# First MLP of a fused attention and two-MLP kernel: the integer addition of the weight conversion from GpSimd to VectorE, r*r on ScalarE in all blocks, and conversion steps left out at three f-steps of a block

## The chip, the cores and the metric

One core of a Trainium2 chip. The metric is the device time of one execution in microseconds, the median of repeated runs. The kernel before takes 1394.09 us (three runs, 1392.44 to 1394.47).

## The reference, cut to what matters

Inputs are float32; the weights arrive as float64 and are taken apart on the chip.

```python
scores = scale * x @ state.T          # per batch and head; S = 512, Ns = 32, D = 64
xread  = softmax(scores)  @ state
sread  = softmax(scores.T) @ x
x = concat([xread, sread])            # 4608 tokens of 512
h = x @ w_in                          # first MLP, 512 -> 2048
r = maximum(h, 0.0)
g = r * r
x = g @ w_out                         # 2048 -> 512
...                                   # second MLP: elu between two products
```

## The kernel before, in words

The program has two stages. The first holds the attention and the first MLP, the second (from about 725 us) the second MLP in a form with seven products. The change touches the first stage alone.

The first stage runs over nine blocks `b`: eight of 512 token columns (kind "X", one batch each) and one of 256 state columns (kind "S"). A block runs over 16 f-steps `i` of 128 hidden units. In an f-step TensorE multiplies for `h` (`s1_x`: six matmuls, each factor split into a high and a low fp32r part, so three matmuls per product), then `relu2` makes the square, and two f-steps later (`LAG = 2`) twelve matmuls add the square times the weights `v1` into four accumulators `acc`. At the end of a block `L400` on ScalarE and `L398` on VectorE copy the four `acc` tiles into `o` (two buffers), in turn ScalarE, VectorE, ScalarE, VectorE, and SyncE stores each.

`relu2` (L355 to L365) is: `r = relu(h)` on ScalarE (L357); `g = r*r` in fp32, on ScalarE in block 0 (L360) and on VectorE in all other blocks (L362); `gs[HI] = r*r` rounded to fp32r on ScalarE (L364); `gs[LO] = g - gs[HI]` on VectorE (L365). `r` and `g` have one buffer each, `gs` has three.

The weights are converted from float64 to float32 by integer work on their two 32-bit words (`convert`, L126 to L144): ScalarE scales the high word (L136) and the low word (L137), VectorE clamps and shifts (L139, L140), GpSimd adds the low word as a 32-bit integer (L142), and VectorE puts the sign in (L144). Each piece is 128x512; there are 64: 16 of `w1`, 16 of `v1`, 16 each of `w2` and `v2`. `w1` and `v1` are used in the first MLP and are converted before and during block 0. `w2` and `v2` go in pairs through `conv_pair`, which also forms sums of quarters (L177 to L181), splits them (L188 on ScalarE, L189 on VectorE) and stores them to HBM for the second stage.

`raw` has four buffers (`RAW = 4`): a piece is loaded by SyncE (L122) when an earlier piece has been given up by L144. `convert` and its callers are generators; each call of `next_conv` takes every conversion in progress one `yield` further. Calls stand in the f-steps: two per f-step in block 0, one in each of the f-steps 2 to 17 of the blocks 1 to 7, until nothing is left to convert. Beside them stand the steps of the attention for the next block (`at_scores`, `at_soft1`, ... , `emit_m`).

The order of instructions on each engine is not that of the code: a scheduler sets it when the program is built. Each engine then works through its own queue in order, and SyncE's queue of DMA issues too.

Of the kernel before, what the change touches and what calls it, by code (L numbers as in the profile page):

```python
# [13 lines left out]
AF = mybir.ActivationFunctionType  # L14
ALU = mybir.AluOpType
# [23 lines left out]
def attn_mlp_kernel(ctx: ExitStack, tc: tile.TileContext, xt, xn, st, w1, v1, w2, v2, outx, outs):  # L39
# [13 lines left out]
    nc = tc.nc  # L53
# [44 lines left out]
    if True:  # L98
# [28 lines left out]
        def convert(name, i, out):  # L127

            t = raw.pop((name, i))
            low, high = t[:, :, 0], t[:, :, 1]
            bits = out.bitcast(I32)
            with tc.issue_after(pace[0].ins) if name in ("w2", "v2") else nullcontext():
                nc.scalar.activation(out=out, in_=high.bitcast(F32), func=AF.Copy, scale=2.0 ** -112)  # L136
            nc.scalar.activation(out=low, in_=low.bitcast(U32), func=AF.Copy, scale=2.0 ** -29)  # L137
            yield
            nc.vector.tensor_scalar(out=out, in0=out, scalar1=CLAMP, scalar2=-CLAMP, op0=ALU.min, op1=ALU.max)  # L139
            nc.vector.tensor_single_scalar(out=bits, in_=bits, scalar=3, op=ALU.logical_shift_left)  # L140
            yield
            nc.gpsimd.tensor_tensor(out=bits, in0=bits, in1=low, op=ALU.add)  # L142
            yield
            nc.vector.scalar_tensor_tensor(out=bits, in0=high, scalar=SIGN, in1=bits, op0=ALU.bitwise_and, op1=ALU.bitwise_or)  # L144

# [206 lines left out]
            for k in range(KC):  # L352
                mm3(ps, (w[:, HI, k], w[:, LO, k]), (op[:, HI, k], op[:, LO, k]), k == 0, k == KC - 1)

        def relu2(ps, n, act):  # L355
            r = g_p.tile([P, n], F32, name="r", tag="r")
            pace[:] = [nc.scalar.activation(out=r, in_=ps, func=AF.Relu)]  # L357
            g = g_p.tile([P, n], F32, name="g", tag="g")
            if act:
                nc.scalar.activation(out=g, in_=r, func=AF.Square)  # L360
            else:
                nc.vector.tensor_tensor(out=g, in0=r, in1=r, op=ALU.mult)  # L362
            gs = gs_p.tile([P, 2, n], F32R, name="gs", tag="gs")
            nc.scalar.activation(out=gs[:, HI], in_=r, func=AF.Square)  # L364
            nc.vector.tensor_tensor(out=gs[:, LO], in0=g, in1=gs[:, HI].bitcast(F32), op=ALU.subtract)  # L365
            return gs

        def block(kind, b, op, bg, nxt):


            n = S if b < B else NST
            gs, acc = {}, []
            for i in range(FC + LAG):
                if i < FC:
                    ps = ps_s1.tile([P, n], F32, name="h", tag="s1")
                    if kind == "X":
                        s1_x(b, op, i, ps)
                    else:
                        s1_s(op, i, ps)
                    gs[i] = relu2(ps, n, kind == "X" and b == 0)  # L380
                for todo in bg.get(i, ()):
                    todo()
                if i == FC - 1:
                    following = nxt()
                f = i - LAG
                if f < 0:
                    continue
                if f == 0:
                    acc = [ps_acc.tile([P, n], F32, name="acc", tag="acc") for _ in range(KC)]
                g = gs.pop(f)  # L390
                w = wo_t["v1", f]
                for k in range(KC):
                    sl = slice(k * P, (k + 1) * P)
                    mm3(acc[k], (w[:, HI, sl], w[:, LO, sl]), (g[:, HI], g[:, LO]), f == 0, f == FC - 1)
            for k in range(KC):
                o = o_p.tile([P, n], F32, name="o", tag="o")
                if k % 2:
                    nc.vector.tensor_copy(out=o, in_=acc[k])  # L398
                else:
                    nc.scalar.activation(out=o, in_=acc[k], func=AF.Copy)  # L400
                nc.sync.dma_start(out=x2d[b][:, k], in_=o)
            return following
# [20 lines left out]
        op = operand_x(0)  # L423

        for b in range(B + 1):
            bg = {i: [] for i in range(FC + LAG)}

            def at(i, fn, *a):
                bg[i].append(lambda: fn(*a))

            nb = b + 1
            if b == 0:
                for i in range(FC - 1):
                    at(i, next_conv)
                    at(i, next_conv)
                at(3, emit_m, 0, 1)
                at(7, emit_m, 0, 2)
                at(11, emit_m, 0, 3)
                at(1, at_sread, 0)
                at(2, at_srt, 0)  # L440
                at(0, load_x, 1)
                at(3, load_xn, 1)
            elif b < B:
                at(1, emit_m, b, 1)
                at(5, emit_m, b, 2)
                at(9, emit_m, b, 3)
                for i in range(2, 18):
                    at(i, next_conv)
            if nb < B:
                at(1 if b else 6, at_scores, nb)  # L450
                at(2 if b else 7, at_soft1, nb)
# [16 lines left out]
            op = block("S" if b == B else "X", b, op, bg, nxt)  # L468
# [18 lines left out]
    act, tt = nc.scalar.activation, nc.vector.tensor_tensor  # L487
# [248 lines left out]
    for n in range(B // 2):  # L736
        g = {}
# [51 lines left out]
```

## Time and profile before

| | |
|---|---|
| median of three runs | 1394.09 us (1392.44 to 1394.47) |
| profiled execution, its own time | 1390.73 us |
| its span, first to last instruction | 1389.0 us |
| TensorE busy | 1330.5 us (96%) |
| VectorE busy | 956.7 us (69%) |
| ScalarE busy | 762.3 us (55%) |
| GpSimd busy | 108.3 us (8%) |
| mean granted TensorE clock | 0.99 |

Matmuls overlap in the profile, so a busy TensorE is not one at its peak; where it waits shows in idle time ahead of an instruction and in what ended that. Busy time in a list of instructions by line counts each in full; in the table by stretch, overlapping ends count once. The arrow behind an idle time names what ended it, as inferred from semaphores.

### The profile page before, as it was taken

The numbers are of one execution on the slowest core, as the hardware profiler recorded it, in microseconds if no ns is written. First come the engines' busy times: TensorE is split into PE (matmuls) and PEld (weight loads), VectorE is DVE, ScalarE is ACT, GpSimd is POOL, SyncE is SP. The second block draws the span as 40 slices with busy tenths as digits, with TensorE's granted clock in tenths as the row PEclk, the third lists the DMA queues.
The fourth block names the chain that finished last, engine by engine and source line by source line (L and its number), as shares of the span: only waits on it lengthen the run. The fifth ranks groups of instructions, "written<-read, shape, count | busy, mean of one in ns | idle before, by whom it ended". The sixth has DMA issues, their size and how long they took to land.

```text
span 1389.0 us, 19369 instructions
## 1 busy us (share of the span) xinstructions
PE 1330.5 (96%) x6992; PEld 1053.9 (76%) x6992; DVE 956.7 (69%) x1387; ACT 762.3 (55%) x1268; POOL 108.3 (8%) x70
## 2 busy tenths in 40 slices
PE   4789998989989999999999999999999999999998
PEld 1556675767767777777898888888888888888898
DVE  7998968788786646443745796469736895468644
ACT  4786655455564434333536764467436754476444
POOL 3443121121201000000000000000000000000000
PEclk8999999999999999999999999999999999999999
DMA  6556555665454210010137687767776677768733
GB/s 244 188 172 211 205 193 205 228 221 213 169 205 154 76 34 31 31 62 1 61 122 208 194 257 217 224 195 221 239 238 192 189 227 221 210 194 283 228 115 105
DMA packets 105071, 242.45 MB, mean 175 GB/s; under 512 B 11664, under 2 KB 13712, under 8 KB 101904
## 3 DMA queue, kind: packets, MB, share of 16 engines
q1 hardware_dynamic: 104976, 241.22, 54.0%
q8 instruction: 55, 0.90, 0.3%
q14 instruction: 40, 0.33, 0.1%
HBM read 185.60 MB, written 55.57 MB: 174 GB/s over the span
## 4 chain that ended last, share of the span: by engine, by line
PE 78%; DVE 7%; issue 3%; DMA 2%; ACT 1%; POOL 1%; DVEq 0%; SPq 0%; POOLq 0%; ACTq 0%
PE acc L85 6%; PE acc L87 6%; PE acc L86 6%; PE X L493 4%; PE x L493 4%; PE x L494 4%; PE X L495 4%; PE X L494 4%; PE x L495 4%; PE h L87 3%; PE h L85 3%; PE h L86 3%; PE Z L495 2%; PE z L494 2%; PE z L493 2%
## 5 line engine op out<-in xcount | busy, mean ns | idle before, releaser
L85 PE MATMUL acc<-gs,v 128*128 128x512 f32 (+1 forms) x576 | 224.4, 390 | 12.1 <-DVE gs L365 12.0
L87 PE MATMUL acc<-gs,v 128*128 128x512 f32 (+1 forms) x576 | 220.3, 382 | 0.0
L86 PE MATMUL acc<-gs,v 128*128 128x512 f32 (+1 forms) x576 | 219.7, 381 | 0.0
L357 ACT ACTIVATE r<-h 128x512 f32<-128x512 f32 (+1 forms) x144 | 82.3, 572 | 215.7 <-PE h L87 147.2
L94 DVE TENSOR_TENSOR gp<-g,gp 128x1024 fp32r<-128x1024 f32 x112 | 136.9, 1223 | 75.7 <-ACT gp L91 74.6
L91 ACT ACTIVATE gp<-g 128x1024 fp32r<-128x1024 f32 x112 | 118.5, 1058 | 110.6 <-PE x L495 62.8
L362 DVE TENSOR_TENSOR g<-r 128x512 f32<-128x512 f32 (+1 forms) x128 | 85.0, 664 | 127.7 <-ACT r L357 126.8
L85 PEld LDWEIGHTS acc<-gs,v 128*128 128x128 f32 x576 | 109.2, 190 | 55.1 <-DVE gs L365 16.9
L87 PEld LDWEIGHTS acc<-gs,v 128*128 128x128 f32 x576 | 109.1, 189 | 26.9 <-issue 6.6
L86 PEld LDWEIGHTS acc<-gs,v 128*128 128x128 f32 x576 | 109.2, 190 | 23.7 <-issue 4.2
L502 DVE SCALAR_TENSOR_TENSOR g<-r,g 128x512 f32<-128x512 f32 x96 | 63.8, 688 | 68.9 <-ACT r L501 68.9
L85 PE MATMUL h<-at,m 128*128 128x512 f32 x256 | 101.8, 398 | 5.5 <-ACT r L357 4.2
L365 DVE TENSOR_TENSOR gs<-g,gs 128x512 fp32r<-128x512 f32 (+1 forms) x144 | 99.6, 692 | 7.2 <-issue 0.2
L87 PE MATMUL h<-at,m 128*128 128x512 f32 x256 | 100.6, 396 | 1.6 <-DVE m L94 1.6
L86 PE MATMUL h<-at,m 128*128 128x512 f32 x256 | 100.7, 393 | 0.0
L493 PE MATMUL X<-xf,wr 128*128 128x512 f32 x256 | 100.3, 392 | 0.0
L494 PE MATMUL x<-gp,wr 128*128 128x512 f32 x256 | 99.7, 389 | 0.0
L495 PE MATMUL X<-xf,wr 128*128 128x512 f32 x256 | 99.6, 389 | 0.0
L495 PE MATMUL x<-gp,wr 128*128 128x512 f32 x256 | 99.6, 389 | 0.0
L494 PE MATMUL X<-xf,wr 128*128 128x512 f32 x256 | 99.6, 389 | 0.0
L493 PE MATMUL x<-gp,wr 128*128 128x512 f32 x256 | 99.6, 391 | 0.0
L500 ACT ACTIVATE r<-g 128x512 f32<-128x512 f32 x96 | 57.5, 625 | 61.4 <-DVE g L579 44.2
(155 smaller groups left out, 2796.2 us busy)
## 6 DMA issues: line engine op xcount, KB each, us to landing
wr<-f_w SPq DMA_DIRECT2D x224, 256.0 KB, 2.9
wr<-f_v SPq DMA_DIRECT2D x224, 256.0 KB, 3.0
raw_w<-in_w_dram SPq DMA_DIRECT2D x32, 512.0 KB, 4.8
raw_v<-in_v_dram SPq DMA_DIRECT2D x32, 512.0 KB, 4.7
f_w<-wf SPq DMA_DIRECT2D x24, 512.0 KB, 2.7
f_v<-wf SPq DMA_DIRECT2D x24, 512.0 KB, 2.6
xt<-in_xt_dram SPq DMA_DIRECT2D x8, 1024.0 KB, 5.2
xn<-in_xn_dram SPq DMA_DIRECT2D x8, 1024.0 KB, 6.6
```

The lines of the kernel that those rows point to most:

```text
L85: mm(ps, w[HI], x[LO], start=first, stop=False)
L86: mm(ps, w[HI], x[HI], start=False, stop=False)
L87: mm(ps, w[LO], x[HI], start=False, stop=last)
L91: nc.scalar.activation(out=hi, in_=src, func=AF.Copy)
L94: nc.vector.tensor_tensor(out=lo, in0=src, in1=hi.bitcast(F32), op=ALU.subtract)
L357: pace[:] = [nc.scalar.activation(out=r, in_=ps, func=AF.Relu)]
L362: nc.vector.tensor_tensor(out=g, in0=r, in1=r, op=ALU.mult)
L365: nc.vector.tensor_tensor(out=gs[:, LO], in0=g, in1=gs[:, HI].bitcast(F32), op=ALU.subtract)
L493: mm(ps, wk[HI], xk[LO], start=start and k == 0, stop=False, skip_group_check=True)
L494: mm(ps, wk[HI], xk[HI], start=False, stop=False, skip_group_check=True)
L495: mm(ps, wk[LO], xk[HI], start=False, stop=last and k == len(w) - 1, skip_group_check=True)
L502: nc.vector.scalar_tensor_tensor(out=out, in0=r, scalar=-1.0, in1=h, op0=ALU.add, op1=ALU.max)
```

## The change

It issues the integer addition of `convert` on VectorE instead of GpSimd, computes `g = r*r` on ScalarE in every block, and in the blocks 1 to 7 leaves out the call of `next_conv` in the f-steps 5, 10 and 15, so that 13 calls stand in a block instead of 16.

```diff
@@ convert
-            nc.gpsimd.tensor_tensor(out=bits, in0=bits, in1=low, op=ALU.add)
+            nc.vector.tensor_tensor(out=bits, in0=bits, in1=low, op=ALU.add)
@@ relu2
-        def relu2(ps, n, act):
+        def relu2(ps, n):
             r = g_p.tile([P, n], F32, name="r", tag="r")
             pace[:] = [nc.scalar.activation(out=r, in_=ps, func=AF.Relu)]
             g = g_p.tile([P, n], F32, name="g", tag="g")
-            if act:
-                nc.scalar.activation(out=g, in_=r, func=AF.Square)
-            else:
-                nc.vector.tensor_tensor(out=g, in0=r, in1=r, op=ALU.mult)
+            nc.scalar.activation(out=g, in_=r, func=AF.Square)
@@ block
-                    gs[i] = relu2(ps, n, kind == "X" and b == 0)
+                    gs[i] = relu2(ps, n)
@@ the loop over blocks, b from 1 to 7
                 for i in range(2, 18):
-                    at(i, next_conv)
+                    if i % 5:
+                        at(i, next_conv)
```

Behind the edit line numbers fall by two to three: L365 becomes L362, L360 becomes L359, L364 becomes L361, L398 and L400 become L395 and L397. L136 to L144 stay.

VectorE in block 0, where `w1` and `v1` are converted (`cv` is a piece of `v1` or `w2`, `w1_..` a piece of `w1`, `raw_..` its two words, `gs` the split square). Before, the addition is in GpSimd's queue and not here:

```order
L140 TENSOR_SCALAR cv_528<-cv_528 128x512
L144 SCALAR_TENSOR_TENSOR w1_20_417<-raw_w19_459,w1_20_417 128x512
L139 TENSOR_SCALAR w1_21_537<-w1_21_537 128x512
L144 SCALAR_TENSOR_TENSOR cv_528<-raw_v16_520,cv_528 128x512
L365 TENSOR_TENSOR gs_516<-g_514,gs_516 128x512
L140 TENSOR_SCALAR w1_21_537<-w1_21_537 128x512
```

Now:

```order
L140 TENSOR_SCALAR cv_528<-cv_528 128x512
L161 TENSOR_TENSOR v1_5_532<-cv_464,v1_5_532 128x512
L144 SCALAR_TENSOR_TENSOR w1_20_417<-raw_w19_459,w1_20_417 128x512
L142 ISA cv_528<-raw_v16_520,cv_528 128x1024
L362 TENSOR_TENSOR gs_563<-g_561,gs_563 128x512
L139 TENSOR_SCALAR w1_21_537<-w1_21_537 128x512
L144 SCALAR_TENSOR_TENSOR cv_528<-raw_v16_520,cv_528 128x512
```

The addition stands in VectorE's own queue, as one instruction of its own kind (ISA) per piece, whose size is given as 128x1024 where the int32 operation had 128x512. There are 64 of them, 36 ahead of the end of block 0.

ScalarE where block 1 ends and block 2 begins (`o` are the copies of the accumulators of block 1, `r` and `gs` behind them are of block 2, `m2` and `at2` operands of its products). Before:

```order
L136 ACTIVATE cv_1917<-raw_w213_1912 128x512
L91 ACTIVATE at2_1922<-atf2_1508 128x512 x2
L400 ACTIVATE o_1980<-acc_1321 128x512
L137 ACTIVATE raw_w26_2214<-raw_w26_2214 128x512
L137 ACTIVATE raw_w214_2216<-raw_w214_2216 128x512
L400 ACTIVATE o_1986<-acc_1323 128x512
L357 ACTIVATE r_1999<-h_1992 128x512
L364 ACTIVATE gs_2003<-r_1999 128x512
L357 ACTIVATE r_2013<-h_2006 128x512
```

Now:

```order
L136 ACTIVATE cv_1909<-raw_w24_1901 128x512
L136 ACTIVATE cv_1910<-raw_w212_1903 128x512
L397 ACTIVATE o_1947<-acc_1321 128x512
L188 ACTIVATE wf_1927<-tf_1768 128x2x256
L357 ACTIVATE r_1966<-h_1959 128x512
L397 ACTIVATE o_1953<-acc_1323 128x512
L359 ACTIVATE g_1968<-r_1966 128x512
L361 ACTIVATE gs_1970<-r_1966 128x512
L357 ACTIVATE r_1980<-h_1973 128x512
```

The two L137, which read pieces of `w2` that have just been loaded, no longer stand between the two copies `o`; the first `r` of the next block stands ahead of the second copy, and each `r` is followed by `g` and `gs` on ScalarE. Before, the same two L137 stand between the copies at the ends of the blocks 2 and 3 too.

ScalarE where block 3 ends and block 4 begins, now:

```order
L136 ACTIVATE cv_3381<-raw_v23_3375 128x512
L136 ACTIVATE cv_3382<-raw_v211_3377 128x512
L137 ACTIVATE raw_v24_3729<-raw_v24_3729 128x512
L137 ACTIVATE raw_v212_3731<-raw_v212_3731 128x512
L397 ACTIVATE o_3423<-acc_2784 128x512
L357 ACTIVATE r_3442<-h_3435 128x512
L397 ACTIVATE o_3429<-acc_2786 128x512
```

Here the two L137 of the next pair still stand at the block's end, ahead of the first copy. Conversions now reach into block 5: 6, 6, 8, 6 and 2 additions lie in the blocks 1 to 5 of VectorE's queue, where before 8, 8, 8 and 4 lay in the blocks 1 to 4.

## Rows read from the trace of the kernel before

**Rows 1.** First line of the profile.

```profile
span 1389.0 us, 19369 instructions
```

**Rows 2.** Busy time by stretch: block 0; 1; 2 to 4; 5; 7 us of block 2.

```profile
core 0: us, PE busy (x) PEld busy (x) DVE busy (x) ACT busy (x) POOL busy (x), PEclk, DMA share, GB/s
35.00:133.30 98.30, 83.53 (x430) 54.35 (x429) 95.62 (x154) 76.57 (x139) 44.25 (x29) 0.99 0.56 188
133.30:210.30 77.00, 74.79 (x443) 56.45 (x442) 61.39 (x113) 43.88 (x81) 11.62 (x6) 1.00 0.56 204
210.30:456.90 246.60, 231.36 (x1328) 171.52 (x1327) 193.31 (x347) 131.57 (x241) 40.49 (x22) 0.97 0.54 196
456.90:532.50 75.60, 74.84 (x443) 56.46 (x443) 39.03 (x62) 29.18 (x51) 0.00 (x0) 1.00 0.13 44
221.00:228.00 7.00, 5.98 (x24) 2.73 (x25) 5.59 (x11) 4.90 (x11) 0.00 (x0) 0.51 0.78 255
```

**Rows 3.** Instructions in order of time, ScalarE, from the end of block 1.

```profile
start us, us, engine line op out<-in xcount [idle before <-releaser]
210.35 0.60 ACT L400 ACTIVATE o<-acc 128x512 f32<-128x512 f32 x1 [2.28 <-PE acc L87]
214.28 0.67 ACT L137 ACTIVATE raw_w<-raw_w 128x512 int32<-128x512 uint32 x1 [3.34 <-DMA raw_w<-in_w_dram]
215.51 0.71 ACT L137 ACTIVATE raw_w<-raw_w 128x512 int32<-128x512 uint32 x1 [0.56 <-DMA raw_w<-in_w_dram]
216.20 0.60 ACT L400 ACTIVATE o<-acc 128x512 f32<-128x512 f32 x1
```

**Rows 4.** The same order of time, VectorE and TensorE behind it.

```profile
214.31 1.78 DVE L144 SCALAR_TENSOR_TENSOR cv<-raw_w,cv 128x512 int32<-128x512 int32 x1 [1.20 <-POOL cv L142]
...
218.90 0.69 DVE L398 COPY o<-acc 128x512 f32<-128x512 f32 x1 [1.61 <-DMA x2d<-o]
...
217.34 0.50 PE L85 MATMUL h<-at,m 128*128 128x512 f32 x1 [1.25 <-ACT r L357]
221.03 0.78 PE L85 MATMUL acc<-gs,v 128*128 128x512 f32 x1 [2.04 <-DVE gs L365]
```

**Rows 5.** ScalarE's copies at the end of block 4.

```profile
456.92 0.60 ACT L400 ACTIVATE o<-acc 128x512 f32<-128x512 f32 x1 [3.40 <-PE acc L87]
459.99 0.60 ACT L400 ACTIVATE o<-acc 128x512 f32<-128x512 f32 x1 [2.48 <-DMA x2d<-o]
```

**Rows 6.** VectorE by line, 35 to 133.3 us: busy us, mean ns of one.

```profile
L365 DVE TENSOR_TENSOR gs<-g,gs 128x512 fp32r<-128x512 f32 x16 | 16.1, 1007 | 0.2 <-issue 0.2
L161 DVE TENSOR_TENSOR v<-cv,v 128x512 fp32r<-128x512 f32 x15 | 14.3, 953 | 0.0
L139 DVE TENSOR_SCALAR cv<-cv 128x512 f32<-128x512 f32 x18 | 12.3, 694 | 1.1 <-ACT cv L136 1.0
...
L140 DVE TENSOR_SCALAR cv<-cv 128x512 int32<-128x512 int32 x18 | 9.3, 526 | 0.1
L144 DVE SCALAR_TENSOR_TENSOR w<-raw_w,w 128x512 int32<-128x512 int32 x11 | 8.6, 778 | 1.2 <-POOL w L142 1.2
L139 DVE TENSOR_SCALAR w<-w 128x512 f32<-128x512 f32 x11 | 7.3, 663 | 0.0
```

**Rows 7.** The same lines by tile over the span: ns, least, median, most.

```profile
L139 DVE TENSOR_SCALAR cv<-cv x48: 406/418/1546, 20.4 to 417.6; 128x512 f32<-128x512 f32 x48
L140 DVE TENSOR_SCALAR cv<-cv x48: 406/416/1430, 20.9 to 418.3; 128x512 int32<-128x512 int32 x48
L144 DVE SCALAR_TENSOR_TENSOR cv<-raw_v,cv x32: 662/679/1781, 29.2 to 423.5; 128x512 int32<-128x512 int32 x32
L161 DVE TENSOR_TENSOR v<-cv,v x16: 674/679/1801, 32.5 to 121.8; 128x512 fp32r<-128x512 f32 x16
```

**Rows 8.** VectorE by line in block 5 (456.9 to 532.5 us), no conversions.

```profile
L365 DVE TENSOR_TENSOR gs<-g,gs 128x512 fp32r<-128x512 f32 x16 | 11.1, 692 | 1.7
L362 DVE TENSOR_TENSOR g<-r 128x512 f32<-128x512 f32 x16 | 11.0, 690 | 24.5 <-ACT r L357 24.3
```

**Rows 9.** By line: a VectorE operation over 128x1024, and block 0's square on ScalarE.

```profile
L265 DVE TENSOR_TENSOR t<-t,m 128x1024 f32<-128x1024 f32 x8 | 9.9, 1241 | 0.0
...
L360 ACT ACTIVATE g<-r 128x512 f32<-128x512 f32 x16 | 10.0, 627 | 4.3 <-DVE gs L365 4.2
```

## The prediction
> **What bounds the kernel now.** I read the table of busy time by stretch first, cut where a block's first accumulator copy begins [rows 2]. It shows three kinds of block. Block 5 converts nothing and takes 75.6 us; TensorE works for 74.8 of them, so this is the floor of a block with the attention beside it. The blocks 2 to 4 convert `w2` and `v2` and take 246.6 us together, 82.2 each: 6.6 us over the floor, 19.8 in all. Block 1 converts as much and takes 77.0, only 1.4 over. Block 0 takes 98.3 us, and there VectorE is busy for 95.6 of them: it is the bound, not TensorE.
>
> Next I read order of time at the end of block 1, to see why blocks 2 to 4 differ from block 1. ScalarE copies its first accumulator at 210.35. Behind it in its queue stands L137, which waits 3.34 us for a load of `raw`, and a second L137 that waits 0.56 more; the second copy starts at 216.20, 5.85 us after the first [rows 3]. At the end of block 4, where no conversion stands between the copies, it is 3.07 us [rows 5]. VectorE is late at the same place for another reason: its L144 waits 1.20 us for GpSimd's addition and then takes 1.78 us instead of 0.68, so that its last copy starts at 218.90 [rows 4, 7]. Behind the copies wait the first squares of block 2: TensorE idles 1.25 us for `r` and 2.04 us for `gs` [rows 4]. Right after that idle time the granted clock is 0.51 for 7 us [rows 2], the 1.2 GHz level; these cost about half of 7 us, 3.4. 1.25 + 2.04 + 3.4 is 6.7, which is the 6.6 of the table. So what the conversions cost the blocks 2 to 4 is a stall at the block's edge, not a lack of throughput: VectorE is busy for 193.3 of 246.6 us and ScalarE for 131.6 [rows 2].
>
> The rest of the span of 1389.0 us [rows 1] is blocks without conversions and the second MLP; the change adds nothing there that TensorE would wait for, and I count them as they are.
>
> **The change part by part.**
>
> *The addition on VectorE, block 0.* GpSimd's additions are not free for VectorE today: instructions that run beside them are stretched. 16 of L365 take 1007 ns on average against 692 in block 5: 5.0 us. 15 of L161 take 953 against a median of 679: 4.1. L139 takes 694 (18 times) and 663 (11 times) against 418: 5.0 and 2.7. L140, 18 times 526 against 416: 2.0. L144, 11 times 778 against 679: 1.1 [rows 6 to 8]. Together 19.9 us, and 1.2 us of waiting for GpSimd [rows 6], 21.1 in all, go away with 29 additions [rows 2]. What comes is 29 additions in VectorE's own queue. The trace has no such instruction. From below: L144 reads the same strided words and the same 128x512 tile, 0.66 us at least, 0.68 in the median [rows 7]. From above: the order gives the instruction 1024 elements, and a two-input operation over 128x1024 takes 1.24 us [rows 9]. I take 0.75, near L144, because the bytes and the access are L144's. 29 x 0.75 = 21.8, so block 0 changes by 21.8 - 21.1 = **+0.7 us**. The ends are 29 x 0.66 - 21.1 = -2.0 and 29 x 1.24 - 21.1 = +14.9. As VectorE is the bound here, nothing covers this term; the few additions ahead of 35 us go the same way and are taken as even.
>
> The Trainium skill (VectorE: DVE Perf Modes, the walkthrough of the modes) says that a two-input operation passes two elements a cycle when all operands are 16-bit with step one, and one otherwise. If the 1024 elements are 16-bit halves in step one, an estimate by its figures is 0.69 us, and the sum for block 0 would be -1.1; if the strided words spoil that, 1.22 us and +14.3. No row here shows which.
>
> *r*r on ScalarE, blocks 1 to 8.* It takes 16 x 0.69 = 11.0 us per block off VectorE [rows 8] and puts 16 x 0.627 = 10.0 us on ScalarE [rows 9]. ScalarE is busy for 131.6 / 3 = 43.9 us per block [rows 2]; 53.9 of 75.6 is cover enough. VectorE goes from 64.4 to 53.4, and with some seven additions of 0.75 to 58.7. As throughput the part costs nothing. As latency it makes ScalarE do `r`, `g` and `gs` one after the other, 0.6 us more before VectorE's subtraction; the squares are used two f-steps later, and a converting f-step is over 4 us (75.6 / 16). It also swaps a wait: `r` no longer waits for VectorE to have read it, but `g` on ScalarE waits until VectorE has subtracted the last one. Queued behind a waiting `g` are the rounding, the next `r`, and the conversions. In block 0, where it is so already, these waits are 4.2 us in 98 with VectorE full [rows 9, 2]; in blocks where VectorE has 17 us to spare I count them at nothing, and if that cover is gone it is rival 2.
>
> The Trainium skill (ScalarE: Activation LUTs, rules for kernel authors) speaks against this part: multiplications belong on VectorE, which it puts at up to three times faster per element in bf16. For fp32 the rows differ: 627 ns on ScalarE, 690 on VectorE. At the rule's full factor ScalarE would carry 43.9 + 33 = 77 us in a 75.6 us block and bind; by the rows it does not, so it gets no chance of its own.
>
> *The thinner steps.* Instructions stay the same, 36 additions ahead of block 1 and 28 behind it; they end in block 5 instead of block 4, long before the second MLP reads their results. What counts is what then stands at a block's edge. At the end of block 1 the two L137 are gone from between the copies (the order above), and at the end of block 2 only one stands ahead of them, for a piece whose neighbour was read some f-step earlier. At the end of block 3 both still stand ahead of the first copy. At the end of block 4 conversions stand there newly, without L137.
>
> *The sum.* Where the load wait is gone, a converting block should look like block 1 or better, since VectorE also loses the 1.20 us wait, the stretch to 1.78, and eleven us of squares; I leave half of block 1's 1.4 us, 0.7. Block 1: -0.7. Blocks 2 and 3: 2 x (6.6 - 0.7) = -11.8. Block 4, with its load wait still there but ahead of the copies: half of 6.6, -3.3. Block 5, now converting: +0.7. Block 0: +0.7. Together **-14.4 us**. The profiled execution took 1390.73 us and would take 1376.3; the median of the runs, 1394.09, lies 3.4 us higher, and the forecast for it is 1394.1 - 14.4 = **1379.7 us**.
>
> **The rivals.**
>
> 1. *All edge stalls go.* Then 19.8 + 1.4 us are won, and with the cheap addition 2.0 more: -23.2, 1370.9 us. For it: half of the stall is the lower clock, and a shorter idle time may not bring the clock down at all (block 5's edge does not). Against: the loads at the end of block 3.
>
> 2. *The wait moves to ScalarE: slower.* ScalarE's queue now holds everything on the way from `h` to `gs` but the last step, and the conversions' loads are waited for in that same queue. If a load of `raw` lands after ScalarE has got to its L136 or L137, the edges of four blocks stall (1 to 4) instead of three: 4 x 6.6 against 19.8, +6.6, and block 0's +0.7: 1401.4 us. The point from which it decides is the first copy of a block's edge: the load must have landed by then. Before, at the end of block 1, it landed 3.9 us behind it (210.35 to 214.28) [rows 3]. For it: the order at the end of block 3, and `g`'s one buffer. Against: at the other three ends the L137 are gone or come earlier.
>
> 3. *The addition is dear.* At 1.24 us block 0 loses 14.9 and not 0.7, which eats the edges' gain: -14.4 + 14.2 = -0.2, 1393.9 us, no change.
>
> That the change does not do what it says is excluded: the order has 64 single additions on VectorE and none left on GpSimd.
>
> **How the numbers follow.** The forecast, with more or less of it at the third edge, has 0.58; rival 1 0.16; rival 2 0.13; rival 3 0.13. A measurement can tell about 0.2% from no change here, 2.8 us. Faster by more: 0.74; within: 0.13; slower: 0.13. The range reaches from rival 1 to the dear addition, 1370 to 1393 us, and leaves rival 2 out.
>
> **What would show it.** Right: blocks 2 and 3 at 76 to 77 us, no stretch at 1.2 GHz behind their edges, 3 to 4 us between ScalarE's two copies, no VectorE row with a mean far over its median, block 0 at 97 to 100 us with VectorE full, the addition at 0.7 to 0.8 us. Wrong: an addition near 1.2 us and block 0 over 105; or `r` at the edges waiting for a load through ScalarE's queue, with the clock still falling. The step that I trust least is what is left of the third edge.

## The result, and the profile after the change

The changed kernel takes 1368.82 us (median of four runs, 1366.99 to 1369.93) against 1393.26 us for the kernel before on the same chip (four runs, 1389.99 to 1394.47). The ratio is 0.9827, with a 95% interval of 0.9806 to 0.9848: 24.4 us faster. The prediction had the sign right, but said 1379.7 us and a range from 1370; the result lies 1.2 us below that range. The profiled execution took 1369.32 us. Its page, in the lines that answer to the table of before:

```profile
span 1367.5 us, 19182 instructions
...
PE 1327.9 (97%) x6992; PEld 1050.9 (77%) x6992; DVE 881.5 (64%) x1323; ACT 823.4 (60%) x1396; POOL 0.7 (0%) x6
```

The span is 21.5 us shorter than that of before [rows 1]. VectorE has lost 75 us of busy time although it has taken on 64 additions, and GpSimd is idle. Busy time by stretch, cut where a block's first accumulator copy starts (blocks 0 to 5):

```profile
core 0: us, PE busy (x) PEld busy (x) DVE busy (x) ACT busy (x) POOL busy (x), PEclk, DMA share, GB/s
...
35.00:128.70 93.70, 84.81 (x437) 52.97 (x436) 89.91 (x181) 76.08 (x136) 0.00 (x0) 1.00 0.58 190
128.70:203.10 74.40, 73.98 (x432) 56.16 (x432) 48.31 (x91) 49.16 (x94) 0.00 (x0) 1.00 0.50 184
203.10:281.50 78.40, 75.22 (x444) 56.43 (x443) 53.21 (x102) 49.53 (x94) 0.00 (x0) 1.00 0.53 190
281.50:359.90 78.40, 76.36 (x450) 57.61 (x449) 54.98 (x106) 51.32 (x96) 0.00 (x0) 1.00 0.53 196
359.90:434.90 75.00, 73.43 (x437) 55.28 (x436) 48.49 (x91) 49.01 (x93) 0.00 (x0) 1.00 0.48 172
434.90:510.90 76.00, 75.02 (x443) 56.44 (x442) 44.84 (x82) 44.00 (x82) 0.00 (x0) 1.00 0.37 137
```

Against before, block 0 ends at 128.7 instead of 133.3 us (-4.5, unrounded), and the blocks 1 to 5 take 74.4, 78.4, 78.4, 75.0 and 76.0 us instead of 77.1, 82.4, 82.1, 82.1 and 75.6 (-2.7, -4.0, -3.7, -7.1, +0.4). Part of what lies between the blocks 1 and 2 is only where the boundary falls: TensorE has 432 instructions in one and 444 in the other. The rest of the span is +0.2. The granted clock is 1.00 in every stretch, where before it fell to 0.51 for 7 us behind the end of block 1 [rows 2], and to 0.52 for 3.5 us and 0.57 for 4.0 us behind the ends of the blocks 2 and 3.

The rows say what the blocks 1 to 5 have won. TensorE is busy for 374.0 of their 382.2 us and idle for 8.2; before, it was busy for 381.0 of 399.2 us and idle for 18.2 [rows 2]. So 10.0 us are idle time, and 7.0 us are busy time, about what the stretches at the lower clock had cost (half of 7 + 3.5 + 4.0 us).

The end of block 1 in order of time, ScalarE and then VectorE (the columns are those of rows 3). VectorE's first copy there before was:

```profile
216.01 0.68 DVE L398 COPY o<-acc 128x512 f32<-128x512 f32 x1
```

Now:

```profile
203.10 0.60 ACT L397 ACTIVATE o<-acc 128x512 f32<-128x512 f32 x1 [1.21 <-PE acc L87]
...
206.99 0.59 ACT L397 ACTIVATE o<-acc 128x512 f32<-128x512 f32 x1
...
203.99 0.68 DVE L395 COPY o<-acc 128x512 f32<-128x512 f32 x1
...
206.12 0.68 DVE L142 CUSTOM_DVE_ANT_0 cv<-raw_w,cv 128x1024 uint16<-128x1024 uint16 x1
206.73 1.28 DVE L144 SCALAR_TENSOR_TENSOR cv<-raw_w,cv 128x512 int32<-128x512 int32 x2
207.94 0.68 DVE L395 COPY o<-acc 128x512 f32<-128x512 f32 x1
```

VectorE runs here without a pause. Its first copy starts 0.9 us after ScalarE's, where before it was 5.7 (216.01 less 210.35), and ScalarE's second copy starts 3.9 us after its first, where before it was 5.85 [rows 3, 4]. VectorE by line in block 0 (35 to 128.7 us), in the columns of rows 6:

```profile
L362 DVE TENSOR_TENSOR gs<-g,gs 128x512 fp32r<-128x512 f32 x16 | 11.0, 685 | 3.9 <-ACT gs L361 3.8
L161 DVE TENSOR_TENSOR v<-cv,v 128x512 fp32r<-128x512 f32 x15 | 10.2, 683 | 0.0
L142 DVE CUSTOM_DVE_ANT_0 cv<-raw_v,cv 128x1024 uint16<-128x1024 uint16 x14 | 9.6, 689 | 0.0
...
L142 DVE CUSTOM_DVE_ANT_0 w<-raw_w,w 128x1024 uint16<-128x1024 uint16 x11 | 7.6, 689 | 0.0
L139 DVE TENSOR_SCALAR cv<-cv 128x512 f32<-128x512 f32 x18 | 7.5, 424 | 0.3 <-ACT cv L136 0.3
```

The stretch is gone: L362, L161 and L139 take 685, 683 and 424 ns where they took 1007, 953 and 694 [rows 6]. The addition takes 0.68 to 0.69 us, the price of L144 [rows 7], and the 29 of them last 19.8 us together. They take less of VectorE's queue than that, because an instruction starts before the one ahead of it has ended: behind 28 of the 29 the next one follows at once, on average 0.60 us after the addition's start (206.12 and 206.73 above).

### The profile page after: what moved, and what is told of

The parts are those of the page before. It is cut to its first block, busy times and chain, and to the rows that moved or that the text cites. A ratio compares the mean times of both kernels' runs of the same rounds, so it can differ in the third digit from the quotient of the medians.

```text
span 1367.5 us, 19182 instructions
## 1 busy us (share of the span) xinstructions
PE 1327.9 (97%) x6992; PEld 1050.9 (77%) x6992; DVE 881.5 (64%) x1323; ACT 823.4 (60%) x1396; POOL 0.7 (0%) x6
## 4 chain that ended last, share of the span: by engine, by line
PE 81%; DVE 5%; ACT 3%; issue 1%; DMA 1%; SPq 0%; ACTq 0%; DVEq 0%
PE acc L85 7%; PE acc L87 7%; PE acc L86 6%; PE x L491 4%; PE X L491 4%; PE X L493 4%; PE X L492 4%; PE x L493 4%; PE x L492 4%; PE h L85 3%; PE h L87 3%; PE h L86 3%; PE z L493 2%; PE Z L493 2%; PE z L491 2%; PE Z L491 2%
## 5 line engine op out<-in xcount | busy, mean ns | idle before, releaser
L357 ACT ACTIVATE r<-h 128x512 f32<-128x512 f32 (+1 forms) x144 | 82.5, 573 | 163.1 <-PE h L87 162.8
L362 DVE TENSOR_TENSOR gs<-g,gs 128x512 fp32r<-128x512 f32 (+1 forms) x144 | 94.8, 658 | 127.1 <-ACT gs L361 121.4
L359 ACT ACTIVATE g<-r 128x512 f32<-128x512 f32 (+1 forms) x144 | 86.9, 603 | 2.0
```

## The experiments

Block times are from the profiled executions, cut as above but not rounded; times and ratios are from repeated runs beside the kernel before on the same chip, whose median there was 1390.9 to 1393.3 us. Each row of block times is one execution, and executions of the kernel before on one chip lie up to 5.8 us apart (1389.04 to 1394.84), so a microsecond or two in one block is not evidence by itself.

| run | median us | ratio, 95% interval | block 0 ends | blocks 1 to 5 | sum |
|---|---|---|---|---|---|
| before | 1393.26 | | 133.3 | 77.1 82.4 82.1 82.1 75.6 | 399.3 |
| after | 1368.82 | 0.9827 (0.9806 to 0.9848) | 128.7 | 74.3 78.4 78.4 75.0 76.0 | 382.1 |
| add_only | 1369.38 | 0.9839 (0.9819 to 0.986) | 129.5 | 74.9 77.5 76.4 78.4 75.6 | 382.8 |
| square_only | 1395.66 | 1.0023 (1.0009 to 1.0038) | 132.3 | 78.4 83.8 81.3 81.7 75.8 | 401.0 |
| thin_only | 1392.13 | 1.0006 (0.9994 to 1.0018) | 134.5 | 81.2 79.7 79.2 78.4 79.0 | 397.4 |
| add_late | 1372.85 | 0.9881 (0.9861 to 0.99) | 134.1 | 76.0 76.3 76.3 76.1 75.6 | 380.3 |
| add_early | 1386.36 | 0.9964 (0.9953 to 0.9975) | 130.8 | 77.2 82.3 82.1 82.0 75.6 | 399.1 |
| beside | 1396.11 | 1.0026 (1.0015 to 1.0036) | 156.9 | 73.9 78.1 78.2 75.0 76.0 | 381.2 |
| twice | 1392.54 | 1.0015 (1.0004 to 1.0025) | 148.5 | 75.3 79.1 78.2 78.6 75.9 | 387.1 |
| raw6 | 1392.04 | 1.0003 (0.9994 to 1.0013) | 134.0 | 77.8 83.2 82.8 82.1 75.6 | 401.5 |
| paced | 1392.94 | 1.001 (1.0001 to 1.002) | 134.3 | 79.0 82.5 82.1 82.1 75.6 | 401.4 |
| edge_only | 1388.96 | 0.9973 (0.9962 to 0.9984) | 134.1 | 77.8 79.9 79.0 81.5 80.1 | 398.3 |
| late_sign | 1391.94 | 0.9999 (0.9987 to 1.001) | 135.7 | 77.1 83.3 80.5 83.2 75.6 | 399.7 |
| add_paced | 1366.96 | 0.983 (0.9816 to 0.9844) | 128.1 | 74.8 76.8 77.2 77.0 75.6 | 381.5 |
| all_paced | 1366.65 | 0.9828 (0.9814 to 0.9842) | 128.9 | 74.7 75.7 75.9 77.6 76.3 | 380.3 |
| add_thin | 1365.73 | 0.9823 (0.9808 to 0.9837) | 129.1 | 74.1 75.8 75.6 77.4 76.1 | 379.0 |

### One part of the change alone

**add_only**, the kernel before with the addition on VectorE:

```diff
-            nc.gpsimd.tensor_tensor(out=bits, in0=bits, in1=low, op=ALU.add)
+            nc.vector.tensor_tensor(out=bits, in0=bits, in1=low, op=ALU.add)
```

> Of the three parts only the addition on VectorE. Theory 1 (the edge theory: block 0 gains because nothing on GpSimd stretches VectorE any more, the later blocks gain where no load of raw is waited for in ScalarE's queue at a block's edge): block 0 ends 4 to 5 us earlier as in the full change; at the edges 1 to 3 the two L137 still stand around the first copy, so the blocks 2 to 4 lose only the wait for GpSimd and the stretched L144, 2 us each; -11 us in all. Theory 2 (relief: the later blocks gain because VectorE has r*r no more): -4 to -5, block 0 alone. Theory 3 (GpSimd alone is to blame for everything): -18 to -21.

**square_only**, the kernel before with `r*r` on ScalarE in every block:

```diff
-                    gs[i] = relu2(ps, n, kind == "X" and b == 0)
+                    gs[i] = relu2(ps, n, True)
```

> Only r*r on ScalarE in all blocks. Theory 1: block 0 unchanged, the L137 stand at the edges as before and ScalarE still waits for the load; 0 to -4 us. Theory 2: the blocks 1 to 4 gain what they gain in the full change, -16. Theory 3: 0.

**thin_only**, the kernel before with fewer conversion steps:

```diff
                 for i in range(2, 18):
-                    at(i, next_conv)
+                    if i % 5:
+                        at(i, next_conv)
```

> Only the thinner steps. Theory 1: the L137 are gone from the edges 1 and 2, one of them stands between the copies at edge 3; blocks 2 and 3 lose about 4 us each, block 4 two, block 0 nothing: -10 us. Theories 2 and 3: within 2 us of before, VectorE and GpSimd do the same work.

Measured: the addition alone brings nearly the whole gain (0.9839 against 0.9827, intervals that overlap), 22.7 us. That is nearest to theory 3; theory 1, the edge theory, had 11. And it does so with the L137 where they were. ScalarE in order of time in add_only, at the end of block 1:

```profile
204.40 0.59 ACT L400 ACTIVATE o<-acc 128x512 f32<-128x512 f32 x1
207.57 0.68 ACT L137 ACTIVATE raw_w<-raw_w 128x512 int32<-128x512 uint32 x1 [2.58 <-DMA raw_w<-in_w_dram]
...
208.62 0.59 ACT L400 ACTIVATE o<-acc 128x512 f32<-128x512 f32 x1
```

The load is still waited for between the copies, 2.58 us here and 2.00 and 3.27 at the ends of the blocks 2 and 3, and still the clock stays at 1.00 behind the first two edges; it falls once, behind the third (0.76 in the mean of 366 to 373 us). The square alone makes the kernel 0.2% slower, which no theory had. The thin steps alone do nothing (theory 1 had -10 us), in an instructive way: the blocks 2 to 4 get 2.7 to 3.7 us shorter, as their edges should, but block 1 gets 4.1 us longer, block 5 3.4 and block 0 1.2. In this one execution the delay does not go with the conversions that leave the edge; it turns up elsewhere, as in block 1, where VectorE's L144 waits 1.19 and 1.20 us for GpSimd at 174.6 and 182.6 us and TensorE then idles 2.80 us for `m` at 187.4. At the ends of the blocks 1 and 2 both the L137 and the L144 that waits are gone here, so these two edges do not tell the one from the other.

### Early and late additions

**add_late** moves only the additions of `w2` and `v2`, **add_early** only those of `w1` and `v1`:

```diff
-            nc.gpsimd.tensor_tensor(out=bits, in0=bits, in1=low, op=ALU.add)
+            (nc.vector if name in ("w2", "v2") else nc.gpsimd).tensor_tensor(out=bits, in0=bits, in1=low, op=ALU.add)
```

> The addition on VectorE for w2 and v2 alone (the pieces that go in pairs, nearly all converted in the blocks 1 to 4); GpSimd keeps w1 and v1. If the two gains of the moved addition are separate, block 0 stays at its end near 133 us and the blocks 1 to 4 take what they take with all additions moved (74.9, 77.5, 76.4, 78.4 us): -16 us, 1376. If the later gain only comes of starting block 1 in better order, -5 or less.

> The mirror: VectorE adds for w1 and v1, GpSimd for w2 and v2. If the gains are separate: block 0 ends 3 to 4 us earlier (four additions of its end stay on GpSimd), the blocks 2 to 4 stay near 82 us; -4 us, 1388.

The two gains are separate, and near what was expected for that case (-16 and -4 us). The late additions bring 18.7 us (1391.54 to 1372.85), all behind block 0: its blocks 1 to 4 take 76.0 to 76.3 us. The early ones bring 5.2 (1391.54 to 1386.36); in the profiled execution block 0 ends 2.5 us earlier and the later blocks are as before, so it does not show where the rest lies. The late gain, the larger one, lies in the blocks 1 to 4.

### GpSimd's company, and the price of an addition

**beside** is the changed kernel, with the same addition done by GpSimd a second time into a tile that nobody reads, so that GpSimd works beside VectorE as before, and only the next load into the buffer of `raw` waits for it (the tile's declaration is left out):

```diff
             nc.vector.tensor_tensor(out=bits, in0=bits, in1=low, op=ALU.add)
+            nc.gpsimd.tensor_tensor(out=idle, in0=idle, in1=low, op=ALU.add)
```

**twice** is the changed kernel with each addition done a second time on VectorE, into an unused tile (its declaration is left out):

```diff
+            nc.vector.tensor_tensor(out=extra, in0=bits, in1=low, op=ALU.add)
             nc.vector.tensor_tensor(out=bits, in0=bits, in1=low, op=ALU.add)
```

> The full change, and beside each of the 64 additions on VectorE one on GpSimd of the same strided words into a tile that nobody reads: work added, nothing waits for it but itself and the buffer of raw. Theory 1 (stretch by company): VectorE's instructions beside it are stretched again as before, some 20 us in block 0, where VectorE is full; block 0 ends 15 to 20 us later than in the full change, the later blocks are up to 1 us longer each; +20 us against the full change. Rival (block 0 gained because VectorE waits for GpSimd no more): 0 to +2 us, with VectorE's durations near their medians.

> The full change with each addition done twice on VectorE, the first time into a tile that nobody reads. If VectorE is the bound of block 0: 29 x 0.685 = +20 us there. If the later blocks have the room that the busy time shows: 0 to +2 us in the blocks 1 to 5 together, as VectorE waits there for nothing from another engine. +20 to +22 us against the full change, 1390. If load on VectorE at the edges is what stalls them, the blocks 2 to 4 go up by 2 us each or more.

Busy time in the profile of beside (columns as above): block 0, then the blocks 1 and 4.

```profile
35.00:156.90 121.90, 99.14 (x449) 61.44 (x450) 120.15 (x190) 78.89 (x139) 56.75 (x30) 0.90 0.49 156
...
156.90:230.80 73.90, 73.47 (x430) 55.79 (x429) 50.38 (x90) 49.05 (x94) 10.80 (x8) 1.00 0.51 186
...
387.10:462.10 75.00, 73.65 (x438) 55.51 (x437) 50.80 (x91) 48.70 (x92) 10.73 (x8) 1.00 0.49 173
```

Block 0 ends 28.2 us later than in the changed kernel, with VectorE busy for 120.15 of 121.90 us: there VectorE is the bound, and company that stretches its instructions is paid in full. In the blocks 1 to 4 GpSimd works for 39.6 us (10.80, 9.20, 8.91, 10.73) and costs nothing; the blocks take what they take without it, although one sign instruction is stretched to 1.79 us right behind the end of block 3, at 388.81. So company accounts for block 0, and in the later blocks company alone is not enough. What is left for them is the hand-over, VectorE's wait for the sum, which this kernel does not have. VectorE by line in the same block 0:

```profile
L145 DVE CUSTOM_DVE_ANT_0 cv<-raw_v,cv 128x1024 uint16<-128x1024 uint16 x15 | 17.9, 1196 | 0.0
L165 DVE TENSOR_TENSOR v<-cv,v 128x512 fp32r<-128x512 f32 x16 | 16.8, 1049 | 0.0
...
L143 DVE TENSOR_SCALAR cv<-cv 128x512 int32<-128x512 int32 x19 | 11.1, 589 | 0.0
```

These are 689, 683 and 422 ns without GpSimd. Not every row is stretched: the subtraction into `gs` has 681 ns here. The Trainium skill (GPSIMD Engine Reference, Key points) says that GpSimd shares its SBUF interfaces with VectorE, and that VectorE's instructions contend that have two SBUF inputs or run in a 2-port perf mode. The two two-input rows shown agree; the one-input row L143 is stretched as well, and the trace does not name the mode that it runs in.

In twice, block 0 ends 19.7 us later, with 36 more additions ahead of its end: 0.55 us each, less than the 0.69 us that one lasts. At 0.60 us from start to start they take 21.7 us of the queue, and VectorE's idle time behind 35 us falls from 3.8 to 1.9 us. The 20 us expected came out by luck, from 29 additions at their full length. In the later blocks the 28 extra ones cost 5.0 us together, 3.6 of it in block 4, where 0 to 2 were expected.

### The load that ScalarE waits for

**raw6** gives `raw` six buffers instead of four, so that loads could start earlier. **paced** holds L137 behind the last `relu`, as L136 already is, so that none can stand between the copies:

```diff
-RAW, CV = 4, 4
+RAW, CV = 6, 4
```

```diff
             with tc.issue_after(pace[0].ins) if name in ("w2", "v2") else nullcontext():
                 nc.scalar.activation(out=out, in_=high.bitcast(F32), func=AF.Copy, scale=2.0 ** -112)
-            nc.scalar.activation(out=low, in_=low.bitcast(U32), func=AF.Copy, scale=2.0 ** -29)
+                nc.scalar.activation(out=low, in_=low.bitcast(U32), func=AF.Copy, scale=2.0 ** -29)
```

> The kernel before with six raw buffers instead of four, so that loads of weights are issued two pieces earlier; GpSimd still adds. Theory A (the edge stall is ScalarE's wait for the load of raw): the loads have landed, the blocks 2 to 4 fall to 76 to 78 us, -12 to -18 us in all. Theory B (the edge stall is VectorE's in-order queue, held by L144 that waits for GpSimd's sum, with the accumulator copies behind it): VectorE's first copy still starts over 4 us behind ScalarE's, the blocks 2 to 4 stay over 80 us; 0 to -4 us.

> The kernel before, GpSimd adding, with one edit on ScalarE: L137 is held behind the same relu as L136 is, so that no L137 stands between the accumulator copies at the edges 1 to 3; VectorE's order there is as before (L144, copy, L144, copy behind GpSimd's sums). Theory A (ScalarE's wait for the load of raw makes the stall): the blocks 2 to 4 fall from 82 to 76 to 78 us, -13 to -18 us. Theory B (VectorE's queue, held by L144 for GpSimd): VectorE's first copy still starts over 5 us behind ScalarE's; the idle time of TensorE for r goes (1.2 us an edge), that for gs and the low clock stay: 0 to -6 us.

raw6 did not do what it was for: at the three edges L137 still waits 3.4, 3.1 and 3.7 us for its load, so it says nothing on the theories. It was the queue and not the buffers that set when the load starts. The issues on SyncE's queue in the kernel before, ahead of the L137 of rows 3:

```profile
205.55 2.22 SPq L174 DMA_DIRECT2D d_w<-cv  x2
208.66 0.32 SPq L190 DMA_DIRECT2D f_w<-wf  x1
209.07 1.22 SPq L122 DMA_DIRECT2D raw_w<-in_w_dram  x2
```

The two loads are issued at 209.07, behind the stores of the last pair, whose tiles VectorE's L144 and L189 finish late (this L144, at 206.7 us, has waited 1.21 us for GpSimd). With six buffers they are issued at 210.57 in a block that ends 1.5 us later, at the same place in the queue.

paced did take the L137 away, and won nothing (1.001). ScalarE, VectorE, TensorE and SyncE's queue at the end of its block 1:

```profile
213.26 0.60 ACT L400 ACTIVATE o<-acc 128x512 f32<-128x512 f32 x1 [1.16 <-PE acc L87]
218.76 0.60 ACT L400 ACTIVATE o<-acc 128x512 f32<-128x512 f32 x1 [4.91 <-DMA x2d<-o]
...
216.88 1.78 DVE L144 SCALAR_TENSOR_TENSOR cv<-raw_w,cv 128x512 int32<-128x512 int32 x1 [1.20 <-POOL cv L142]
...
218.92 0.68 DVE L398 COPY o<-acc 128x512 f32<-128x512 f32 x1
...
219.90 0.50 PE L85 MATMUL h<-at,m 128*128 128x512 f32 x1 [0.90 <-ACT r L357]
223.93 0.50 PE L85 MATMUL acc<-gs,v 128*128 128x512 f32 x1 [2.37 <-DVE gs L365]
...
213.88 0.33 SPq L401 DMA_DIRECT2D x2d<-o  x1
```

Nothing stands between ScalarE's copies, and yet the second starts 5.5 us after the first: a store, that of its first copy (there are two `o` buffers), has taken the load's place. That store is issued as soon as its copy ends and the wait for it lasts 4.91 us, where at an edge without conversions it lasts 2.48 [rows 5]; why it is slower here no run shows. VectorE's copy is as late as before (5.66 us), with the same two marks on L144, 1.20 us of waiting for GpSimd and 1.78 us of duration. As theory B had it, VectorE's first copy is over 5 us late, but of the 1.25 us that TensorE idled for `r`, 0.90 are still there. The load wait was one cover among several, and taking it away alone is worth nothing. Because ScalarE stayed late, this run does not say what its lateness costs by itself; that it is enough to take the hand-over away is shown by add_only, where L137 still waits between the copies.

### Does the place of the wait decide?

My theory was now that VectorE's wait for GpSimd costs time because it lies between the copies. **edge_only** keeps GpSimd and moves the conversions off the edge; **late_sign** keeps everything at the edge and gives the sum one more step to be ready (and takes one step away from the pair's sums of quarters behind it):

```diff
-                for i in range(2, 18):
+                for i in range(2, 15):
```

```diff
             nc.gpsimd.tensor_tensor(out=bits, in0=bits, in1=low, op=ALU.add)
             yield
+            if name in ("w2", "v2"):
+                yield
...
-            yield
```

> The kernel before with no conversion steps in f-steps 15 to 17 of blocks 1 to 7: GpSimd keeps all additions, but no L144 that waits for GpSimd stands between VectorE's two copies any more (and the two L137 stand ahead of the copies at two of the edges). Theory: the stall at a block's end is VectorE's in-order queue held there by that wait, with the copies and the next squares behind it; so blocks 2 to 4 fall from 82 to 76 to 78 us with GpSimd in use, -12 to -18 us, about 1376 us, block 0 as before. Rival (GpSimd's company, or its latency wherever it lies, sets the time): the waits for GpSimd come back at other places and the blocks stay at 80 to 82 us, no change, about 1391 us.

> The kernel before with one more step between GpSimd's addition and the sign (L144) in the pieces of w2 and v2, and one less in the pair behind it: additions stay on GpSimd and the same instructions stand at the edge, with the sums of quarters behind the sign. Theory (VectorE waits for GpSimd between the copies): at the edges L144 still stands between the copies; if it now finds its sum ready, its wait of 1.20 us goes, VectorE's first copy starts within 3 us of ScalarE's instead of 5.67, and blocks 2 to 4 fall by 3 to 6 us each. Rival (the load that L137 waits for, or the stores, set the edge): ScalarE's second copy still starts 5.8 us after its first and the blocks stay at 82 us, about 1391 us.

late_sign missed: its sign instruction still waits 1.20 us between the copies, VectorE's first copy is still 5.64 to 5.66 us late at three edges, so it decides nothing. edge_only did clear the copies: ScalarE's second copy comes 2.8 to 2.9 us after its first at the ends of the blocks 1 to 3, VectorE's first copy at most 0.7 us after ScalarE's. Yet the blocks 1 to 5 take 398.3 us instead of 399.3, the ratio is 0.9973 (about 1376 us were expected, 1388.96 came), and the theory that the wait costs only between the copies falls. VectorE's waits there, over the blocks 1 to 5 (us in all, times, the longest):

```profile
DVE cv L144 <- POOL cv L142: 11.8, 10, 1.2
```

That is as much as in the kernel before (10.2 us in nine waits), and the two marks of rows 4 recur. Order of time in edge_only, VectorE and then TensorE, near the end of block 3 and then in the middle of block 4:

```profile
362.76 1.79 DVE L144 SCALAR_TENSOR_TENSOR cv<-raw_v,cv 128x512 int32<-128x512 int32 x1 [1.20 <-POOL cv L142]
...
365.67 0.68 DVE L365 TENSOR_TENSOR gs<-g,gs 128x512 fp32r<-128x512 f32 x1
...
366.41 0.50 PE L85 MATMUL acc<-gs,v 128*128 128x512 f32 x1 [2.38 <-DVE gs L365]
...
417.69 1.78 DVE L144 SCALAR_TENSOR_TENSOR cv<-raw_v,cv 128x512 int32<-128x512 int32 x1 [1.20 <-POOL cv L142]
...
421.75 1.28 DVE L94 TENSOR_TENSOR m<-mp,m 128x512 fp32r<-128x512 f32 x2
...
422.50 0.41 PE L314 MATMUL srt<-ident,srs 128*64 128x128 f32 x2 [2.80 <-DVE m L94]
```

One such L144 makes VectorE 1.20 + 1.1 = 2.3 us late, and behind it in the queue stand `g`, `gs` or `m`, which TensorE wants; TensorE then idles 2.38 and 2.80 us. Not every wait gets that far. Behind those at 176.2, 270.7 and 409.8 us TensorE does not wait for VectorE, and neither does it in the kernel before behind the three inside the blocks 1, 2 and 4 (175.3, 257.6, 421.8 us). So the wait costs where what stands behind it is due at once: the copies, `g`, `gs` or `m`. The clock falls behind some of these idle times here too (0.98 in the mean of the blocks 2, 4 and 5).

At the end of block 1 edge_only shows another thing. VectorE, SyncE's queue, ScalarE and TensorE:

```profile
207.66 0.69 DVE L144 SCALAR_TENSOR_TENSOR cv<-raw_w,cv 128x512 int32<-128x512 int32 x1 [1.21 <-POOL cv L142]
208.38 0.32 SPq L174 DMA_DIRECT2D d_w<-cv  x1
208.79 1.50 SPq L122 DMA_DIRECT2D raw_w<-in_w_dram  x2
211.95 0.69 DVE L398 COPY o<-acc 128x512 f32<-128x512 f32 x1 [1.19 <-PE acc L87]
213.19 0.66 ACT L137 ACTIVATE raw_w<-raw_w 128x512 int32<-128x512 uint32 x1 [5.83 <-DMA raw_w<-in_w_dram]
213.75 0.58 ACT L400 ACTIVATE o<-acc 128x512 f32<-128x512 f32 x1
217.76 0.50 PE L85 MATMUL h<-at,m 128*128 128x512 f32 x1 [0.75 <-ACT r L357]
221.65 0.83 PE L227 MATMUL sc<-xt,st 64*32 64x512 f32 x1 [1.81 <-DVE m L94]
```

Here VectorE is in time and ScalarE is late: its first copy stands behind an L137 that waits 5.83 us for its load, TensorE idles 0.75 and 1.81 us, and the clock falls to 0.52 from 222 to 225.5 us. So a load wait can cost at an edge by itself. Its start goes back to the hand-over in part: the load stands in SyncE's queue behind the store of a piece whose L144 has waited 1.21 us for GpSimd.

### Versions with the addition on VectorE

**add_paced** and **all_paced** are add_only and the changed kernel with the edit of paced; **add_thin** is the changed kernel with `r*r` left as before (`act` is handed over again as there).

```diff
             g = g_p.tile([P, n], F32, name="g", tag="g")
-            nc.scalar.activation(out=g, in_=r, func=AF.Square)
+            if act:
+                nc.scalar.activation(out=g, in_=r, func=AF.Square)
+            else:
+                nc.vector.tensor_tensor(out=g, in0=r, in1=r, op=ALU.mult)
```

> The addition on VectorE alone, and L137 held behind the relu as L136. If the load waits that are left at the edges (2 to 3 us of ScalarE in the run with the addition alone) still cost something, the blocks 2 to 4 go from 77.5, 76.4, 78.4 to 76 each: 1 to 4 us under that run, 1366 to 1368. If they are covered: 1369 again.

> The full change, and L137 held behind the relu as L136. In the full change the blocks 2 and 3 took 78.4 us, with ScalarE waiting up to 6.5 us for a load within the last f-steps of block 2 (TensorE 2.3 us for gs). If that is these two blocks' rest: 76 each, 3 to 5 us under the full change, 1364 to 1366.

> Addition on VectorE and thinner steps, r*r as before. With the addition alone at 1369.4 and all three at 1368.8 the two other parts are worth nothing once GpSimd is out of the way, whatever they do to the order: 1367 to 1372. If they cancel, this one lies over 3 us to one side.

The three lie within 1.3 us of each other on one chip, with 1365.73 us the lowest, and their ratios of 0.9823 to 0.983 cannot be told from the change's 0.9827. So once the addition has moved, neither the square on ScalarE nor the hold on L137 has a worth of its own that these runs can show. add_paced bears on ScalarE's lateness: its second copy comes 4.7 to 5.1 us after its first at the ends of the blocks 1 to 3, not much less than in paced (5.5 to 6.6), and yet its blocks 2 to 4 take 76.8 to 77.2 us at a clock of 1.00, not 82. One place shows what a load wait can cost. In the changed kernel, ScalarE near the end of block 2, and TensorE behind it:

```profile
276.98 0.66 ACT L137 ACTIVATE raw_v<-raw_v 128x512 int32<-128x512 uint32 x1 [6.47 <-DMA raw_v<-in_v_dram]
...
278.53 0.62 ACT L359 ACTIVATE g<-r 128x512 f32<-128x512 f32 x1
279.05 0.62 ACT L361 ACTIVATE gs<-r 128x512 fp32r<-128x512 f32 x1
...
280.45 0.50 PE L85 MATMUL acc<-gs,v 128*128 128x512 f32 x1 [2.30 <-DVE gs L362]
```

Here a load wait of 6.47 us in ScalarE's queue does reach TensorE, 2.30 us; `g` ahead of `gs` on ScalarE is 0.5 us of that. all_paced, which keeps the square there, and add_thin have the blocks 2 and 3 at 75.6 to 75.9 us instead of 78.4, and give some of it back in block 4 (77.6 and 77.4 instead of 75.0).

## Why the prediction was wrong

The forecast was 10.9 us too high. Of that, 7.0 us is the sum (-14.4 against -21.4 between the profiled executions), and 3.9 is the way from the profiled execution to the median: I added 3.4 us, since that of before lay so far under its median, and that of after lies 0.5 over its own. Of the 7.0 us, 5.2 lie in block 0. For the blocks 1 to 5 the sum said -15.1 us, and -17.2 came: near, but by luck, because the reason given for most of it did not hold.

**The step that failed** is that of the explanation of the edges: "the two L137 are gone from between the copies", taken as what frees an edge, so that the thin steps would bring the gain and only where L137 leaves the copies. paced takes the L137 from between the copies at all three edges, thin_only at two, and neither brings anything (1.001 and 1.0006); add_only leaves one at each, and brings nearly everything (0.9839). I had the other cause in a row, L144's 1.20 us for GpSimd and its 1.78 us [rows 4], and gave it a share of the edge where the hand-over to GpSimd was the root: with VectorE's queue held for 2.3 us per such L144, its copies, `g`, `gs` and `m` come late, and so do the stores and loads that SyncE issues behind them. At the three edges, and at some of the places where edge_only put the waits, that reached TensorE.

The prediction also read one edge for three. Behind the ends of the blocks 2 and 3 the clock fell for 3.5 and 4.0 us and not for 7, and behind each of them TensorE idled another 1.46 us for `m` (0.99 behind the first), which its sum of 6.7 leaves out; that this met the 6.6 of the table was in part chance.

Term by term, forecast and measured:

- Block 0, +0.7, with the start; measured -4.5. The addition lasts 0.687 us on average, not 0.75, and takes 0.60 of the queue: 29 times 0.15 is 4.3. The stretch was 22.1 and not 19.9 us, because my rows left out the rare lines (two L144 at 1229 ns, 0.55 over the median each, L181 at 1330 instead of 414, L265 at 1401 instead of 1241: 2.2). And the stretch ahead of 35 us was not even: the first `h` matmul of block 0 comes at 30.59 instead of 31.65 us, 1.1 earlier. Against these stands VectorE's idle time behind 35 us, which grew from 2.7 to 3.8 us, nearly all of it waiting for ScalarE's `gs`, where I had it fall by 1.2. Even the lower end of -2.0 was too high.
- Block 1, -0.7; measured -2.7. I had taken block 5's 75.6 us as a floor for it; the boundary with block 2 moved.
- Blocks 2 and 3, -11.8; measured -7.7. The old stall went, clock and all, and a new one came in part: the 2.30 us above. The 1.45 us for `m` at 291 us had been there before (1.46 at 305.6).
- Block 4, -3.3; measured -7.1. I had halved it for the load wait at the end of block 3, where "both still stand ahead of the first copy". They stand there, and the clock does not fall.
- Block 5, +0.7; measured +0.4.

**Of the rivals**, the first (all edge stalls go, 1370.9 us) is nearest, with its reason: the idle times that are left do not bring the clock down. The second, the wait that moves to ScalarE, happened once, for 2.30 us, and not at four edges. The third is out: 0.68 us, not 1.24. The estimate of 0.69 us worked out from the Trainium skill (VectorE: DVE Perf Modes, the walkthrough of the modes) was for 16-bit halves in step one; the trace shows uint16 operands and 0.68 us, with the words of `low` strided by the kernel's code.

**Of the signs named beforehand**, right were: no 1.2 GHz stretch, 3 to 4 us between ScalarE's copies (3.9, 4.1, 3.1), no mean far over its median. Wrong were the blocks 2 and 3 (78.4, not 76 to 77), block 0 (93.7 us from 35, not 97 to 100, with VectorE busy for 89.9 of them) and, just, the addition (0.68 to 0.69 us, not 0.7 to 0.8).

What stays open: how much of an edge's stall in the kernel before came through ScalarE's late second copy (held by a load, or in paced by a store) and how much straight from VectorE. add_paced speaks for VectorE, the first edge of edge_only for some share of ScalarE's; no run separates them, and the store that holds ScalarE in paced does not hang on VectorE's queue. How the 2.3 us divide into the wait of 1.20 and the stretch of 1.1 was not separated either. Company of GpSimd beside the kernel with the addition alone, where VectorE still has `r*r`, and GpSimd's addition with the square and the thin steps together were not run.

## What to carry to other kernels

A short operation handed to a helper engine in the middle of a chain is paid for in the queue of the engine that takes the result back: whatever stands behind the wait there is late, and loads and stores that are issued behind it are late too. It costs time where one of these is due at once. When an edge shows two late engines, look for the one whose lateness makes the other's, and try to take away each wait alone before crediting one; a schedule that moves the wait elsewhere can clear the edge that you look at and lose the time at another place. Ask of contention whether the engine that is stretched has time to spare: the same company cost 28 us where VectorE was full and nothing where it was not.

## What had not been expected of the hardware

- The integer addition over 128x512 words on VectorE runs as one instruction on uint16 operands, named 128x1024, and takes 0.68 us, as long as a 512-element operation and half of a two-input one over 128x1024 fp32 [rows 9]; by the kernel's code the words of `low` lie apart by the high words between them, and it does not show in the time.
- GpSimd's work into a private tile, for which VectorE never waits, raised VectorE's subtraction for `v` from 683 to 1049 ns and its additions for `v1` from 689 to 1196, and delayed block 0 by 28.2 us.
- Waits of 2.58 and 2.00 us for loads in ScalarE's queue, between the copies of add_only, left TensorE's clock at 1.00; behind the third, of 3.27 us, it fell. One of 6.47 us in the changed kernel cost TensorE 2.30 us, and its clock did not fall for that.
